# Decode attention beside an MLP on one core: the V loads of pairs 0 to 27 in ScalarE's own DMA queue, ScalarE's program written out

## The chip, the cores and the metric

The kernel runs on 1 of the 8 cores of one Trainium2 chip. A core has five engines with a program each: TensorE (PE in the profile; PEld is its weight load), VectorE (DVE), ScalarE (ACT), GpSimd (POOL) and SyncE (SP), and 16 DMA engines which move data between HBM and the on-chip memory SBUF. The metric is the device time of one execution in microseconds (us).

## The reference

One decode step: attention over a cache of 4096 keys for 8 batches and 32 heads, beside a small MLP on the same normalised input.

```python
# x: [8, 1, 640]; k_cache, v_cache: [8, 32, 4096, 128] bf16
def _A_ref(x, k_cache, v_cache, wq, wo):
    q = (x @ wq).reshape(B, Sq, Hq, Dh).transpose(0, 2, 1, 3)
    scores = jnp.einsum("bhqd,bhkd->bhqk", q, k) * (Dh ** -0.5)
    p = _softmax(scores, axis=-1)
    o = jnp.einsum("bhqk,bhkd->bhqd", p, v)
    return o.transpose(0, 2, 1, 3).reshape(B, Sq, Hq * Dh) @ wo
def _B_ref(x, w1, b1, w2, b2):
    h = _gelu(_layernorm(x) @ w1 + b1)
    return h @ w2 + b2
xn = _layernorm(x)
return x + _A_ref(xn, k_cache, v_cache, wq, wo) + _B_ref(xn, w1, b1, w2, b2)
```

The two caches are 537 MB, the weights 15 MB. Each byte of the caches is used once.

## The kernel before

The work is cut into 32 pairs i = 0 to 31: a group of 8 heads and one batch (`hq, b = divmod(i, 8)`). A pair's K and its V are one load each of 8.39 MB: 128 partitions (8 heads times 16 blocks of keys) of 256 keys of 128 numbers, 64 KB in each partition. SBUF has room for three such tiles in `S_sb`: slots KA and KB take K of even and of odd pairs, and slot VS takes every V. So two K loads can be under way or in use at a time, and one V.

For each pair the scores of the first 176 keys of a partition come from DVE in three chunks (`dve_chunk`: a multiplication by the broadcast query `qbc_sb`, which ScalarE copies from PSUM in `act_qbc`, a halving addition, a sum). The other 80 keys go through PE: `pe_T` transposes them in ten tiles, `act_T` copies each tile out of PSUM, `pe_QK` multiplies, `dve_sel` picks the own head. `k_ready` is a small POOL instruction that waits for the K load and releases PE. `dve_max` makes the maximum, `act_exp` (ScalarE, eight exps) the probabilities, `pe_RS` and `dve_rinv` the sums of them. `pe_PV` (256 matmuls) needs the V load and the probabilities; `act_O` copies its result to `oU_sb`, and `o_norm` on POOL scales it. After pair 31 the selected heads are multiplied by `wo` and the result is stored.

The order on every engine comes from positions: `at(pos, fn, i)` puts a step at a place, the steps are sorted by it, and each engine's instructions are recorded in that order. Pair i begins at i * 100. The places that matter: `load_k(i)` at -51, `act_qbc(i)` at -10.5, `act_T(i)` from 0 to 42, `load_v(i)` at +50, and, for the pair before, `pe_PV(i - 1)` at +50 and `act_O(i - 1)` at +71; `act_exp(i)` is at +90. On ScalarE the order is thus: evictions of pair i, oU copy of pair i - 1, query copy of pair i + 1, exps of pair i. On PE: transposes and scores of pair i, PV of pair i - 1, the query broadcast `pe_qbc` of pair i + 1.

All K and V loads are issued by SP, so they stand in one DMA queue, in SP's order: K of pair i + 1, V of pair i, K of pair i + 2, and so on. `load_k(i)` (line 350) waits until PE and DVE have read the K of pair i - 2; `load_v(i)` (line 362) waits for the end of PV of pair i - 1, since V has one slot. The last V is cut in four pieces. ScalarE issues three small loads at the start (x and the biases) and the store at the end.

SP's and POOL's programs are written out (`_replay`, line 116). DVE and ScalarE run pairs 2 to 31 as a loop of 15 turns of two pairs (`replay`, line 845, and `_replay_loop`, line 151): the recorded turns are compared, and semaphore waits get a register that grows with the turn. PE has a loop of its own (`_replay_pe`). As every instruction is emitted by `_emit`, the profile gives line 111 for all of them; they are told apart by their tiles.

Of the kernel before, what the change touches and what calls it, by code (L numbers as in the profile page):

```python
# [104 lines left out]
def _emit(e, call, wait=None, turn=None):  # L105
    name, a, k, inc = call
    a = [x.at(x.i if turn is None else turn) if isinstance(x, _Slot) else x for x in a]
    if name == "wait_ge":
        e.wait_ge(a[0], a[1] if wait is None else wait, **k)
        return  # L110
    inst = getattr(e, name)(*a, **k)  # L111
    if inc is not None:
        inst.then_inc(*inc)


def _replay(e, calls):
    for call in calls:
        _emit(e, call)
# [32 lines left out]
def _replay_loop(e, calls, a, b, n):  # L151

    size = (b - a) // n
    assert size * n == b - a and n >= 2
    _replay(e, calls[:a])
    grow = _steps([calls[a + r * size:a + (r + 1) * size] for r in range(n)])
    with e.bass.Fori(0, n, engines=OrderedEngineSet([e.engine])) as r:
        for call, step in zip(calls[a:a + size], grow):
            _emit(e, call, call[1][1] + r * step if step else None)
    _replay(e, calls[b:])  # L160
# [31 lines left out]
def bass_parallel_sum__gqa_block_cached__mixer_channel_mlp__decode_kernel(  # L192
# [11 lines left out]
    out: bass.AP,  # L204
):
    B, _, D = A_x.shape
    _, H, SK, DH = A_k_cache.shape
    F = B_w1.shape[1]
    assert DH == P and D % P == 0 and B == 8 and H % 8 == 0 and SK % P == 0
# [4 lines left out]
    NQ = NHQ * B  # L214
# [4 lines left out]
    TPB = 8  # L219
    NS = 2  # L220
    LOOP0, LOOPN = 2, 15
    assert NKEY == 256 and NQ == 32
    SLOT = NKEY * DH
    KA, KB, VS = 0, 1, 2
# [5 lines left out]
    def jp_of(i):  # L230
        return 80
# [16 lines left out]
    with ExitStack() as es:  # L248
# [6 lines left out]
        tile = [S_sb[:, s, :].rearrange("p (j d) -> p j d", d=DH) for s in range(3)]  # L255
# [72 lines left out]
        pe, dve, act, sp, pool = (_Eng(sem(f"{n}_s")) for n in ("pe", "dve", "act", "sp", "pool"))  # L328
        pe2, act2 = _Eng(sem("pe2_s")), _Eng(sem("act2_s"))
        ld_s = [_Dma(sem(f"ld_s{s}")) for s in range(3)]  # L330
# [6 lines left out]
        tk = {}  # L337
        prog = []

        def at(pos, fn, *a):  # L340
            prog.append((pos, len(prog), fn, a))
# [4 lines left out]
        def cache_src(cache, i):  # L346
            hq, b = divmod(i, B)
            return cache[b, hq * HS:(hq + 1) * HS].rearrange("h (p j) d -> (h p) j d", j=NKEY)
# [11 lines left out]
            tk[("k", i)] = ld_s[s].sig(sp.dma_start(tile[s][:, lo:hi, :], cache_src(A_k_cache, i)[:, lo:hi, :]))  # L360

        def load_v(i):
            sp.wait(tk["mlp"] if i == 0 else tk[("pv" if i < NQ - 1 else "pvh", i - 1)])
            if i < NQ - 1:
                tk[("v", i)] = [ld_s[VS].sig(sp.dma_start(tile[VS], cache_src(A_v_cache, i)))]
                return
            tk[("v", i)] = []
            for d, lo, hi in zip([ld_s[VS]] + ld_vl, V_CUT[:-1], V_CUT[1:]):
                if lo:
                    d.n += 1  # L370
                    sp.wait(tk[("pv", i - 1)])
                tk[("v", i)].append(
                    d.sig(sp.dma_start(tile[VS][:, lo:hi, :], cache_src(A_v_cache, i)[:, lo:hi, :])))
# [406 lines left out]
        for i in range(NQ):  # L780
            o = i * Q
            last = i == NQ - 1
            if i:
                at(o - 51, load_k, i)
            at(o + 50, load_v, i)
            at(o - 52, qrep, i)
            at(o - 2, k_ready, i)
            at(o - 11, pe_qbc, i)
            at(o - 10.5, act_qbc, i)
            nt = jp_of(i) // TPB  # L790
            w = 42.0 / nt
            for t in range(nt):
                at(o + w * t, pe_T, i, t)
                at(o + w * (t + 0.4), act_T, i, t)
                at(o + w * (t + 1.5), pe_QK, i, t)
            at(o + 2, dve_chunk, i, 0)
            at(o + 26, dve_chunk, i, 1)
            at(o + 52, dve_sel, i, 0)
            at(o + 55, dve_sel, i, 1)
            at(o + 58, dve_chunk, i, 2)  # L800
            at(o + 84, dve_max, i)
            at(o + 90 if i else o + Q + 45, act_exp, i)
            at(o + Q + 48, pe_RS, i)
            at(o + Q + 57, dve_rinv, i)
            at(o + Q + 50, pe_PV, i)
            if not last:
                at(o + Q + 71, act_O, i)
            at(o + Q + 75, o_norm, i)
# [3 lines left out]
        o = NQ * Q  # L812
# [10 lines left out]
            at(o + 5 if n == 0 else o + 79.2, pe_sel3, n)  # L823
            at(o + 5.5 if n == 0 else o + 79.5, dve_fold3, n)
        at(o + 90, fin_store)
        engs = {"dve": dve, "act": act}
        marks = {n: [] for n in engs}
        for m in range(LOOPN + 1):
            for n in engs:
# [12 lines left out]
        for _, _, fn, a in sorted(prog, key=lambda t: (t[0], t[1])):  # L842
            fn(*a)

        def replay(e, n):
            m = marks[n]
            assert len({y - x for x, y in zip(m, m[1:])}) == 1, (n, m)
            _replay_loop(e, engs[n].calls, m[0], m[-1], LOOPN)

        @block.sync  # L850
        def _(e):
            _replay(e, sp.calls)
# [9 lines left out]

        @block.scalar
        def _(e):
            replay(e, "act")

        @block.gpsimd
        def _(e):
# [29 lines left out]
```

## Time and profile before

| | us |
|---|---|
| median of 3 runs (1283.54 to 1283.78) | 1283.76 |
| the profiled execution | 1283.81 |
| its span, first to last instruction | 1281.8 |
| PE busy | 671.3 (52%) |
| DVE busy | 1095.1 (85%) |
| ScalarE busy | 475.1 (37%) |
| POOL busy | 88.7 (7%) |

The DMA engines moved 551.99 MB at a mean of 431 GB/s. Queue q1 is SP's and carried 551.79 MB; q10 is ScalarE's and carried 0.03 MB. Times in the views below are microseconds from the start of the span. A row of the chain gives start, duration and what; a row of the timeline gives start, duration, engine, operation, output and inputs, and in brackets how long the engine was idle before it and what released it. `SPq` and `ACTq` are DMA issues: their duration is that of the issue, not of the transfer.

### The profile page before, as it was taken

Reading aid. Unit: us, or ns where it says so; the run is one execution under the profiler, and the core shown is the slowest. Engines: PE = TensorE matmul, PEld = TensorE weight load, DVE = VectorE, ACT = ScalarE, POOL = GpSimd, SP = SyncE. Lnnn points to the kernel's source line nnn. Section 1 sums busy time; section 2 is a strip of 40 time slices with the busy share of each in tenths; the row PEclk is TensorE's granted clock in tenths of the full one; section 3 lists DMA queues with packets and bytes.
Section 4 is the critical chain, followed back from the end, with each engine's and each line's share of the span. In section 5 each row is a group of like instructions: output and inputs, shape, how many; then the busy total and the mean of one; then the engine's idle time right before and its main releaser. Section 6 shows DMA issues by size and latency. Waiting matters only on the chain.

```text
span 1281.8 us, 34444 instructions
## 1 busy us (share of the span) xinstructions
PE 671.3 (52%) x13944; PEld 575.0 (45%) x13944; DVE 1095.1 (85%) x675; ACT 475.1 (37%) x904; POOL 88.7 (7%) x108
## 2 busy tenths in 40 slices
PE   4365554564544564544664644654545655545645
PEld 4254443453443553433553534543434544434545
DVE  1799988988888988888988888988889988889885
ACT  1344432344432344423344423344323344323441
POOL 0001000000000000000000000000000000000001
PEclk9955655566655656555655555565555555555555
DMA  9999999999999999999999999999999999999998
GB/s 396 436 439 424 442 427 438 427 442 427 436 429 442 427 436 429 442 427 434 432 442 427 434 432 440 429 434 432 440 430 432 432 442 429 432 432 442 429 417 369
DMA packets 11235, 551.99 MB, mean 431 GB/s; under 512 B 1292, under 2 KB 1493, under 8 KB 1878
## 3 DMA queue, kind: packets, MB, share of 16 engines
q1 hardware_dynamic: 11152, 551.79, 99.7%
q8 instruction: 9, 0.15, 0.0%
q10 hardware_dynamic: 70, 0.03, 0.0%
q14 instruction: 4, 0.03, 0.0%
HBM read 551.80 MB, written 0.01 MB: 430 GB/s over the span
## 4 chain that ended last, share of the span: by engine, by line
DMA 80%; PE 19%; ACT 1%; issue 1%; SPq 0%; another core or an unknown queue 0%; DVE 0%; POOL 0%; ACTq 0%
DMA S_sb<-in_A_v_cache_dram 74%; PE PV_ps L111 17%; DMA S_sb<-in_A_k_cache_dram 3%; DMA S_sb<-in_A_wo_dram 2%; DMA S_sb<-in_B_w_dram 2%; PE TR_ps L111 1%; PE CH_ps L111 1%; ACT P_sb L111 0%; PE ACC_ps L111 0%; SPq L111 0%; PE S_ps L111 0%; ACT KT_sb L111 0%; PE QB_ps L111 0%; ACT S_sb L111 0%
## 5 line engine op out<-in xcount | busy, mean ns | idle before, releaser
L111 PE MATMUL TR_ps<-ident_bf,S_sb 128*128 128x128 bf16 (+1 forms) x2570 | 341.5, 278 | 376.8 <-POOL kr_sb L111 366.0
L111 DVE TENSOR_TENSOR S_sb<-S_sb,qbc_sb 128x7552 bf16<-128x7552 bf16 (+1 forms) x96 | 388.8, 4050 | 136.8 <-DMA S_sb<-in_A_k_cache_dram 136.8
L111 PEld LDWEIGHTS TR_ps<-ident_bf,S_sb 128*128 (+2 forms) x2570 | 244.8, 103 | 434.6 <-issue 360.3
L111 DVE TENSOR_REDUCE Sd_sb<-S_sb 128x59 f32<-128x3776 bf16 (+1 forms) x96 | 390.2, 4065 | 6.0
L111 ACT ACTIVATE KT_sb<-TR_ps 128x1024 bf16<-128x1024 bf16 x320 | 326.9, 1023 | 125.6 <-PE TR_ps L111 115.5
L111 PE MATMUL PV_ps<-P_sb,S_sb 128*128 128x8 bf16 x8192 | 224.0, 175 | 149.3 <-DMA S_sb<-in_A_v_cache_dram 146.2
L111 PEld LDWEIGHTS PV_ps<-P_sb,S_sb 128*128 128x128 bf16 x8192 | 221.2, 103 | 152.2 <-DMA S_sb<-in_A_v_cache_dram 149.0
L111 ACT ACTIVATE P_sb<-Sd_sb,NB_sb 128x256 bf16<-128x256 f32 x256 | 126.2, 494 | 218.5 <-DVE NB_sb L111 218.5
L111 DVE TENSOR_TENSOR S_sb<-S_sb 128x3776 bf16<-128x3776 bf16 (+1 forms) x96 | 202.9, 2114 | 3.3
L111 ACT ACTIVATE oU_sb<-PV_ps 128x8 f32<-128x8 f32 x31 | 5.5, 177 | 393.2 <-PE PV_ps L111 393.2
L111 PE MATMUL S_ps<-qrep_sb,KT_sb 128*128 128x8 bf16 x2560 | 122.0, 177 | 35.5 <-ACT KT_sb L111 31.8
L111 PEld LDWEIGHTS S_ps<-qrep_sb,KT_sb 128*128 128x128 bf16 x2560 | 91.8, 103 | 66.6 <-ACT KT_sb L111 39.5
L111 POOL TENSOR_TENSOR oT_sb<-oU_sb,ri_sb 128x8 bf16<-128x8 f32 x31 | 68.2, 2199 | 389.4 <-DVE S_sb L111 366.1
L111 ACT ACTIVATION_READ_ACCUMULATOR P_sb<-Sd_sb,NB_sb 128x1 f32 x256 | 47.7, 186 | 0.0
L111 POOL COPY qrep_sb<-qT_sb 128x128 bf16<-128x128 bf16 x32 | 14.5, 453 | 455.6 <-PE S_ps L111 435.8
L111 DVE TENSOR_TENSOR S_ps<-S_ps,mask_sb 128x320 f32<-128x320 f32 (+2 forms) x67 | 32.7, 488 | 4.3 <-PE S_ps L111 4.3
L111 DVE TENSOR_REDUCE Sd_sb<-S_ps 128x40 f32<-128x320 f32 x64 | 31.5, 492 | 2.2
L111 POOL MEMSET kr_sb<- 128x1 f32 x32 | 3.1, 98 | 324.0 <-DMA S_sb<-in_A_k_cache_dram 324.0
L111 PE MATMUL CH_ps<-rs_sb,ones_f 128*128 128x8 f32 x64 | 17.3, 344 | 9.9 <-DVE oS_sb L111 6.2
L111 PE MATMUL QB_ps<-ident_bf,qrep_sb 128*128 128x128 bf16 x32 | 9.1, 285 | 22.6 <-DVE S_sb L111 21.5
L111 PEld LDWEIGHTS CH_ps<-rs_sb,ones_f 128*128 128x128 f32 x64 | 15.1, 292 | 10.1 <-DVE oS_sb L111 6.3
L111 ACT ACTIVATE qbc_sb<-QB_ps 128x128 bf16<-128x128 f32 x32 | 8.8, 276 | 27.8 <-PE QB_ps L111 27.8
(57 smaller groups left out, 119.1 us busy)
## 6 DMA issues: line engine op xcount, KB each, us to landing
S_sb<-in_A_wq_dram SPq DMA_DIRECT2D x1, 5120.0 KB, 15.7
S_sb<-in_A_k_cache_dram SPq DMA_DIRECT2D x1, 4448.0 KB, 43.2
S_sb<-in_A_k_cache_dram SPq DMA_DIRECT2D x1, 3744.0 KB, 33.3
S_sb<-in_A_v_cache_dram SPq DMA_DIRECT2D x1, 3072.0 KB, 10.7
S_sb<-in_A_wo_dram SPq DMA_DIRECT2D x1, 2560.0 KB, 31.2
S_sb<-in_A_v_cache_dram SPq DMA_DIRECT2D x1, 2560.0 KB, 12.5
S_sb<-in_B_w_dram SPq DMA_DIRECT2D x1, 2160.0 KB, 20.4
S_sb<-in_B_w_dram SPq DMA_DIRECT2D x1, 2080.0 KB, 25.3
```

What stands on the lines that cost most here:

```text
L111: inst = getattr(e, name)(*a, **k)
```

## The change

`load_v(i)` of pairs 0 to 27 is issued by ScalarE, which waits for the same PV as SP did; V of pairs 28 to 31 stays with SP. The step moves from place +50 to +71.5 for these pairs, which is right behind `act_O(i - 1)` and ahead of `act_qbc(i + 1)` on ScalarE. ScalarE's instructions of different turns are no longer alike, so its program is written out like SP's; DVE keeps its loop. Loads, tiles, slots and semaphores are as before.

```diff
+    V_ACT = 28
@@
         def load_v(i):
-            sp.wait(tk["mlp"] if i == 0 else tk[("pv" if i < NQ - 1 else "pvh", i - 1)])
+            e = act if i < V_ACT else sp
+            e.wait(tk["mlp"] if i == 0 else tk[("pv" if i < NQ - 1 else "pvh", i - 1)])
             if i < NQ - 1:
-                tk[("v", i)] = [ld_s[VS].sig(sp.dma_start(tile[VS], cache_src(A_v_cache, i)))]
+                tk[("v", i)] = [ld_s[VS].sig(e.dma_start(tile[VS], cache_src(A_v_cache, i)))]
                 return
@@
-            at(o + 50, load_v, i)
+            at(o + (71.5 if i < V_ACT else 50), load_v, i)
@@
-        engs = {"dve": dve, "act": act}
+        engs = {"dve": dve}
@@
         @block.scalar
         def _(e):
-            replay(e, "act")
+            _replay(e, act.calls)
```

## The prediction

> **What bounds the kernel now.** I read the page first: how busy the DMA engines are, and whose waits end the chain.
>
> ```profile
> span 1281.8 us, 34444 instructions
> DMA  9999999999999999999999999999999999999998
> q1 hardware_dynamic: 11152, 551.79, 99.7%
> DMA 80%; PE 19%; ACT 1%; issue 1%; SPq 0%; another core or an unknown queue 0%; DVE 0%; POOL 0%; ACTq 0%
> ```
>
> The 16 DMA engines are full in every slice, with one queue, q1, which is SP's. The chain says "PE 19%", but that is the V slot being read between two V loads. The chain in order of time, one pair:
>
> ```profile
> 402.58 31.62 DMA S_sb<-in_A_v_cache_dram
> 434.20 0.05 issue
> 434.25 7.01 PE PV_ps L111 x256
> 441.26 0.02 issue
> 441.28 31.62 DMA S_sb<-in_A_v_cache_dram
> ```
>
> The period is 441.28 - 402.58 = 38.70 us. The timeline of the same stretch shows what the DMA engines do meanwhile:
>
> ```profile
> 402.58 0.33 SPq L111 DMA_DIRECT2D S_sb<-in_A_v_cache_dram  x1
> 402.58 0.18 ACT L111 ACTIVATE oU_sb<-PV_ps 128x8 f32<-128x8 f32 x1 [12.85 <-PE PV_ps L111]
> 403.43 0.28 ACT L111 ACTIVATE qbc_sb<-QB_ps 128x128 bf16<-128x128 f32 x1 [0.67 <-PE QB_ps L111]
> ...
> 409.12 0.33 SPq L111 DMA_DIRECT2D S_sb<-in_A_k_cache_dram  x1
> ...
> 414.89 0.10 POOL L111 MEMSET kr_sb<- 128x1 f32 x1 [9.88 <-DMA S_sb<-in_A_k_cache_dram]
> 414.97 4.03 DVE L111 TENSOR_TENSOR S_sb<-S_sb,qbc_sb 128x7424 bf16<-128x7424 bf16 x1 [4.27 <-DMA S_sb<-in_A_k_cache_dram]
> ...
> 443.68 4.09 DVE L111 TENSOR_REDUCE Sd_sb<-S_sb 128x59 f32<-128x3776 bf16 x1
> ...
> 447.84 0.33 SPq L111 DMA_DIRECT2D S_sb<-in_A_k_cache_dram  x1
> ...
> 453.60 0.10 POOL L111 MEMSET kr_sb<- 128x1 f32 x1 [9.87 <-DMA S_sb<-in_A_k_cache_dram]
> ```
>
> Landings: K 414.89, V 434.20, K 453.60, so 19.35 us each, strictly one after the other. V is asked for at 402.58, stands behind a K load with 12.3 us to go, and lands 31.6 us later. The next K is always asked for (409.12, 447.84) before the V ahead of it has landed, so the one queue never runs dry; during the 7 us of a PV, when no V load can be asked for, a K load is in flight. What bounds the kernel is 551.79 MB at this rate. Nothing can gain unless the rate rises; anything that leaves the DMA engines without a request is lost at full price. The working below therefore counts DMA idle time.
>
> **The change part by part.** E is the end of one PV, T the time to the next one.
>
> Issue moved from SP to ScalarE: SP loses 28 issues of 0.33 us, ScalarE gains them (its own three at the start took 0.61 and 0.54 for two). The new wait for pv stands right behind the oU copy, which waits for the same PV, so it delays nothing by itself. Behind it on ScalarE stand the qbc copy and the exps: qbc waits 0.67 us for PE anyway, which covers 0.33. V is asked for some 0.2 us later than now. Cost nothing; without the cover 28 x 0.33 = 9 us.
>
> K requests no longer stand behind V's wait on SP: they gain nothing. In the rows above K goes out at 447.84, right after the DVE reduce that frees its slot (443.68 + 4.09 = 447.77), 6.5 us after V's issue. DVE, not SP, times it.
>
> V 0 goes out behind ScalarE's evictions of pair 0, at about 61 us in place of 32.12. Then K 1 is in flight (lands 66.3 now) and K 2 is asked for at 71.38. V 0 fills in between: no idle time.
>
> ScalarE without a loop: the branch goes, some 900 instructions are gone through once each. The only idle time that can be code on its way is 3.10 us inside PE's first pass through PV, where PE goes through a matmul in 27 ns (7.00 us for 256). If one such stall fell ahead of every V issue, it cost 28 x 3.10 = 87 us. The nearer row is SP's: its program has no loop today, and its V issues stand 38.70 us apart with no exception; ScalarE has some 28 instructions a pair and waits 12.85 us before every oU, which covers a stall. I take nothing. The Trainium skill (Runtime: NRT & Kernel Launch, Instruction fetch mechanics) says that straight code is prefetched and the crossing mostly hidden; by it the sum is the same.
>
> Two queues in place of one order: this is the step that counts. Do the engines serve ScalarE's queue beside SP's? The first microseconds of the timeline show it:
>
> ```profile
> 0.73 0.38 SPq L111 DMA_DIRECT2D S_sb<-in_A_wq_dram  x1
> 0.74 0.61 ACTq L111 DMA_DIRECT2D S_sb<-in_A_x_dram  x1
> 1.39 0.54 ACTq L111 DMA_DIRECT2D S_sb<-in_B_b_dram  x2
> 2.40 0.87 DVE L111 BATCH_NORM_STATS2 S_sb<-S_sb 8x6 f32<-8x320 bf16 x2 [0.33 <-DMA S_sb<-in_A_x_dram]
> 11.02 0.19 PE L111 MATMUL ACC_ps<-S_sb 128*128 128x40 bf16 x1 [3.33 <-DMA S_sb<-in_B_b_dram]
> 16.46 4.43 PE L111 MATMUL CH_ps<-S_sb 128*128 128x8 bf16 x160 [4.89 <-DMA S_sb<-in_A_wq_dram]
> ```
>
> x, asked for after wq, is in use 1.7 us later; the small biases arrive at 11, before wq at 16.4. So the queues are served in turns, not by order of arrival. How large V's share is the rows don't say (x had hardly to wait, the biases 9 us for 4.6 KB); nothing favours one side, so I take half each. The Trainium skill (DMA: Bandwidth & Descriptors, Queues, rings and completion order) has each DMA engine go round-robin over queues packet by packet; that is the same half, if K and V packets are alike.
>
> Consequence: while both run, V needs up to 38.7 us in place of 19.35. K, which alone has the engines during the 7 us of PV and the start of V, gets 7.05 + 19.35 = 26.4 us of service in 45.8, more than the 19.35 it needs: a K load every 33.6 us, and DVE's 34.5 us a pair (414.97 to the end of its last row at 449.41) is then its limit. K's lead, 12 us short today, is made up in one or two pairs. K loads run ahead, until something else than K's landing holds DVE: the qbc copy. The qbc of pair i+1 comes after PV of pair i-1, so DVE starts a pair at E + 1.2 at the earliest (403.71 + 0.05 against 402.56). Today that is covered, for K lands only at 414.89; it is what is late next. From there: DVE takes 32.80 us to the last reduce (414.97 to 447.77), K is asked for at E + 34.1, and data flow at E + 35.7 (1.6 us from issue to arrival, as x; bounds 1.0, x from the end of its issue, and 3.6, wq's 15.7 to land against 12.1 of work at 19.35 us per 8.39 MB).
>
> Now the balance. K starts at E + 35.7. The next PV ends at E + T, and V's data start 1.8 later; until then K is alone for T - 33.9. Its rest, 19.35 - (T - 33.9) = 53.25 - T, is shared, and V is that much later than alone: V takes 19.35 + 53.25 - T. The next period is 1.8 + 72.6 - T + 7.05 = 81.45 - T. Equal periods: T = 40.7. Check: V lands at E + 33.65 and K starts at E + 35.7; the engines stand still for 2.05 us, and 38.7 + 2.05 = 40.75. The previous K has landed by then. So each of PV 1 to 26 has a hole of 2.05 us: 26 x 2.05 = 53 us. The shares drop out of it: V takes its own 19.35 and whatever K is served before V lands.
>
> Handover: V 28 is SP's again, with K 30 behind it in SP's order. At PV 27 K 29 has landed, K 30 can't be asked for, and the engines are idle for the whole PV and a start: 7.05 + 1.6 = 8.7 us. From there the order is today's.
>
> Sum: 53 + 9 = 62. The profiled execution took 1283.81 us, 0.05 above the median of 1283.76, with a span of 1281.8 and 2.0 around it: 1283.8 + 62 = 1346.
>
> Bounds. The start counts half in every hole and whole at the handover: 1.0 gives -8, 3.6 gives +28. The balance isn't damped (next period 81.45 - T): if a long and a short period alternate, say 46 and 36.5, the short one has a hole of 35.7 - (36.5 - 7.05) = 6.2 us and the long one none: 13 x 6.2 = 81 for 53, +28. With K served at two fifths V takes 32.3 us, K has 7.05 + 12.9 = 20.0 us in 39.3 and gains 1.2 us a pair, so the first ten holes are missing: -20.
>
> **Rivals.** *No change.* The Trainium skill (DMA: Bandwidth & Descriptors, Issuing engines are not separate DMA queues) says that spreading DMAs over issuing engines saves only issue time; by that 1283.8. As a mechanism here: the engines stay full if K never gets ahead. At a K share near three tenths, K gets 7.05 + 0.3 x 27.6 = 15.3 in 34.7 us, less than it needs, so K keeps holding DVE and a K load is in flight in every PV: 1284. For it: x came at once. Against: the biases took 9 us. 0.08.
>
> *Faster.* Two streams move more than one. The rate over a period is 16.78 MB / 38.70 = 433.5 GB/s; single 19 us stretches show up to 443. If the mix held 443 over 28 pairs, 1083 us become 1060: 1261. It has to be above 433.5 by more than the holes cost, 5%, or by 0.24% without holes. Against it: q1 is at 99.7% of the engines already. 0.05.
>
> *Much slower.* The mix loses rate: each per cent costs 11 us on top of 62; 5% gives 1400. ScalarE's stalls, if not covered, give up to 1346 + 87 = 1433. Nothing in the trace shows either. 0.07.
>
> **How the numbers follow.** Holes as worked out: 0.80, likeliest 1346, its own range 1318 to 1395 (1346 - 20 - 8 below; 1346 + 28 and most of the second 28 above). Leaving out no change, faster and most of much slower (0.08 + 0.05 + 0.07 = 0.2) the range is 1295 to 1395; its lower end, with some 12 us of holes left, takes in shares of K between two fifths and three tenths. Within 0.2% (2.6 us) is what a measurement of this kernel can't tell from no change. Faster 0.05; same 0.07; slower 0.88 (0.80, 0.07 and 0.01 of no change that isn't quite).
>
> **What would show it.** In the profile after: a DMA share below 1.0 in 7 us windows over PV; q1 and ScalarE's queue q10 near half of the bytes each; V landing after 30 to 36 us; K landing well before DVE uses it, DVE waiting for qbc (PE, ScalarE) and no longer for K; PV starts 40 to 41 us apart, or alternating around that; one period near 28 us after PV 27, then 38.7 again. K landings that still end DVE's waits would make the prediction wrong, towards no change; DMA engines that are full all the time with longer periods would mean a lost rate.

## The result and the profile after

| | us |
|---|---|
| before, median | 1283.76 |
| after, median | 1363.68 |
| ratio, with its 95% interval | 1.0619 (1.0603 to 1.0635) |
| span before, profiled execution | 1281.8 |
| span after, profiled execution | 1361.2 |

The change makes the kernel 6.2% slower, 79.9 us by the medians. (Two of the six runs after, 1394.63 and 1395.01 us, count as slow and are left out of the ratio; the other four, 1362.55 to 1363.90, give 79.5 us.) First the page of the kernel after, its span and its queues (packets, MB, share of 16 DMA engines over the span):

```profile
span 1361.2 us, 34023 instructions
q1 hardware_dynamic: 7120, 316.90, 55.4%
q10 hardware_dynamic: 4102, 234.91, 39.9%
```

The bytes are the same, split over two queues, and the shares add up to 95.3% where one queue had 99.7%. The timeline of the kernel after, through one period:

```profile
401.93 0.33 ACTq L111 DMA_DIRECT2D S_sb<-in_A_v_cache_dram  x1
402.77 0.28 ACT L111 ACTIVATE qbc_sb<-QB_ps 128x128 bf16<-128x128 f32 x1 [0.67 <-PE QB_ps L111]
403.07 4.03 DVE L111 TENSOR_TENSOR S_sb<-S_sb,qbc_sb 128x7424 bf16<-128x7424 bf16 x1 [5.96 <-ACT qbc_sb L111]
...
431.77 4.09 DVE L111 TENSOR_REDUCE Sd_sb<-S_sb 128x59 f32<-128x3776 bf16 x1
...
435.93 0.33 SPq L111 DMA_DIRECT2D S_sb<-in_A_k_cache_dram  x1
...
436.61 7.00 PE L111 MATMUL PV_ps<-P_sb,S_sb 128*128 128x8 bf16 x256 [16.73 <-DMA S_sb<-in_A_v_cache_dram]
...
443.65 0.18 ACT L111 ACTIVATE oU_sb<-PV_ps 128x8 f32<-128x8 f32 x1 [24.63 <-PE PV_ps L111]
443.65 0.33 ACTq L111 DMA_DIRECT2D S_sb<-in_A_v_cache_dram  x1
```

DVE is now released by the query copy and no longer by K's landing: 403.07 is 1.17 us after the end of PV at 401.90. Its last reduce ends at 435.86, K is asked for at 435.93, and V has landed at 436.57. At that moment the DMA engines have nothing on hand but a request 0.6 us old. The waits of the kernel after say the same for the whole run (who waited for what: us in total, times, longest):

```profile
DVE S_sb L111 <- ACT qbc_sb L111: 191.0, 28, 9.0
DVE S_sb L111 <- DMA S_sb<-in_A_k_cache_dram: 25.8, 3, 15.5
```

Before, the second row read 136.8 us in 30 waits. What the engines do when a V has landed is seen in windows of 5 us; the columns are from:to, length, busy time of PE, PEld, DVE, ACT and POOL, clock, DMA share and GB/s. Before, V landed at 472.90:

```profile
471.00:476.00 5.00, 3.06 (x114) 3.06 (x115) 4.93 (x5) 0.00 (x0) 0.00 (x0) 0.50 1.00 433
```

After, V landed at 477.33 in the first window, and V 27, the last one on ScalarE's queue, at 1218.99, just ahead of the second:

```profile
476.00:481.00 5.00, 3.62 (x135) 3.62 (x136) 3.09 (x7) 0.00 (x0) 0.00 (x0) 0.50 0.61 210
...
1219.00:1226.00 7.00, 6.97 (x256) 6.90 (x256) 1.33 (x6) 0.00 (x0) 0.00 (x0) 0.50 0.00 0
```

433 GB/s against 210: that is the hole; and at the handover nothing moves through a whole PV. (In windows as short as these the DMA column is rough, since packets of 2.42 us lie across their edges.)

Where the 79.4 us of span went, from the ends of PV in the two chains: PV 1 ends 22.5 us later than before (154.16 for 131.65); the 26 periods to PV 27 have a mean of 41.23 us for 38.70, together 65.6; the period after it is 29.16 for 38.69, which gives 9.5 back; the tail takes 0.8. 22.5 + 65.6 - 9.5 + 0.8 = 79.4. Most of the 22.5 us is no loss of its own: K's loads are served ahead there while V waits. The trace's packet records (start, duration, size and queue of each DMA packet, which no view prints) give the other side of it. Counting for each moment which part of the 16 engines had no data packet under way, 65.1 us are lost in the kernel after and 4.2 before; and the packets that start after a hole take about 3.1 us for 64 KB in place of 2.42, worth another 18.4 us. 60.9 + 18.4 = 79.3. For one hole of the long middle that is some 1.8 us without a packet and 0.7 of slow packets. The first ones differ: 2.2 us more than before are lost up to the end of PV 0, and 4.0 in the period that ends with PV 1.

### The profile page after: what moved, and what is told of

Read it like the earlier page. It is cut to its first block, busy times and chain, and to the rows that moved or that the text cites. A ratio compares the mean times of both kernels' runs of the same rounds, so it can differ in the third digit from the quotient of the medians.

```text
span 1361.2 us, 34023 instructions
## 1 busy us (share of the span) xinstructions
PE 675.9 (50%) x13944; PEld 575.0 (42%) x13944; DVE 1095.1 (80%) x675; ACT 465.9 (34%) x904; POOL 24.0 (2%) x108
## 4 chain that ended last, share of the span: by engine, by line
DMA 82%; PE 16%; ACT 1%; issue 1%; SPq 0%; DVE 0%; POOL 0%; ACTq 0%
DMA S_sb<-in_A_v_cache_dram 77%; PE PV_ps L111 16%; DMA S_sb<-in_A_k_cache_dram 3%; DMA S_sb<-in_A_wo_dram 2%; ACT KT_sb L111 1%; SPq L111 0%; PE TR_ps L111 0%; PE ACC_ps L111 0%; PE S_ps L111 0%; PE QB_ps L111 0%; ACT out_sb L111 0%; DVE res_sb L111 0%; ACT oU_sb L111 0%; POOL kr_sb L111 0%; ACTq L109 0%
## 5 line engine op out<-in xcount | busy, mean ns | idle before, releaser
L111 PE MATMUL TR_ps<-ident_bf,S_sb 128*128 128x128 bf16 (+1 forms) x2570 | 341.5, 283 | 64.6 <-POOL kr_sb L111 39.5
L111 ACT ACTIVATE KT_sb<-TR_ps 128x1024 bf16<-128x1024 bf16 x320 | 323.2, 1021 | 99.6 <-PE TR_ps L111 91.3
L111 PEld LDWEIGHTS S_ps<-qrep_sb,KT_sb 128*128 128x128 bf16 x2560 | 92.3, 103 | 146.8 <-DVE S_sb L111 83.6
L111 POOL TENSOR_TENSOR oT_sb<-oU_sb,ri_sb 128x8 bf16<-128x8 f32 x31 | 11.0, 355 | 706.7 <-ACT oU_sb L111 694.6
L111 POOL COPY qrep_sb<-qT_sb 128x128 bf16<-128x128 bf16 x32 | 9.5, 295 | 546.6 <-PE S_ps L111 527.2
L111 PE MATMUL CH_ps<-S_sb 128*128 128x8 bf16 (+1 forms) x244 | 12.0, 181 | 5.1 <-DMA S_sb<-in_A_wq_dram 4.4
## 6 DMA issues: line engine op xcount, KB each, us to landing
S_sb<-in_A_wo_dram SPq DMA_DIRECT2D x1, 2560.0 KB, 31.6
```

## The experiments

My theory: the engines serve the two queues in turns, K runs ahead until the query copy, behind PV, holds DVE, and a hole opens at every PV since K is then asked for too late. Rivals: ScalarE's written-out program; a loss that two queues make in themselves; something that happens once.

**ScalarE's program alone.**

```diff
-    V_ACT = 28
+    V_ACT = 0
```

> All V loads issued by SP again, ScalarE's program still written out without a loop. Theory (the holes come from the two queues): as before, 1283.8 us within 2, V loads 38.70 us apart. Rival (the loss is ScalarE's code on its way, or its program form): most of the 80 us stays, around 1340 to 1365.

Measured: 1287.94 us, ratio 1.0034 (1.0022 to 1.0047). So the form of the program isn't the cause of the 80 us, but it isn't free either, which the theory had missed. The chain of this run shows where the 4.2 us are:

```profile
441.37 31.63 DMA S_sb<-in_A_v_cache_dram
473.00 0.05 issue
473.04 7.01 PE PV_ps L111 x256
480.05 0.02 issue
480.06 32.32 DMA S_sb<-in_A_v_cache_dram
```

Single V loads take 32.3 us in place of 31.6, and little else changes. The page counts 12 code packets in queue q14, 4 before; in the packet records one of them lies in each of the seven longer periods (one 0.35 us longer, six 0.67 to 0.69). Three others, in the periods that end with PV 3, 12 and 23, cost nothing.

**DVE's program written out instead**, with the kernel before and ScalarE's loop as it was:

```diff
-        engs = {"dve": dve, "act": act}
+        engs = {"act": act}
@@
-                replay(e, "dve")
+                _replay(e, dve.calls)
```

> The kernel before, with DVE's program written out in place of ScalarE's; every load as before. If the 4.2 us of the run with ScalarE's program written out are code on its way through the DMA engines (there 7 code packets beyond pair 5 stood in the 7 periods that were 0.35 to 0.69 us longer), DVE, with some 21 instructions a pair for 28, has 4 to 6 such periods: 1286 to 1288. Rival (something of ScalarE's own, its waits or its copies): 1283.8 within 1.

Measured: 1287.78 us, 1.0032 (1.0020 to 1.0043). Nine code packets, and four periods of 39.66 to 39.68 and one of 38.89, for 38.70. So the cost follows written-out code, not ScalarE; the longer step in the chain is the load itself. How one code packet of 8 KB makes a load that 16 engines share 0.7 to 1.0 us longer can be read from the last whole V load, of pair 30, behind which there is little left to load. In the kernel before, its last 16 packets end 0.5 to 2.2 us ahead of the landing. With ScalarE's program written out, one packet ends 0.5 us ahead of the landing, the one before it 2.4 us earlier, as on one engine in sequence, and all others are through 4.8 us or more ahead of it; with DVE's written out, 4.5 us or more. So one engine has fallen behind the rest by some 4 us, about the whole loss, while the others went on to the next loads. The records don't name the engines. But read this way a code packet costs time only where the engine that ends last has served it, which fits the packets that cost nothing, here and in the kernel before (two in its long middle).

**Half the pairs.**

```diff
-    V_ACT = 28
+    V_ACT = 14
```

> V loads of pairs 0 to 13 alone go through ScalarE's queue, 14 to 31 through SP's. Theory (one hole per PV while K is ahead, and one hole of a whole PV at the handover): the loss of 79.9 us falls by 14 holes of 41.23 - 38.70 = 2.53 us, so 79.9 - 35.4 = 44.5: 1328 us. After the handover, periods of 38.70 at once. Rival (something that happens once, at the start or at the handover): the loss stays near 80. Rival (a cost that needs all pairs, ScalarE's code): near 80 too.

Measured: 1330.3 us, 1.0400 (1.0340 to 1.0461); after the handover 29.18, then 38.70 again (39.4 to 39.6 in places, as with the written-out program alone). One of the four runs took 1345.16 us, the others 1329.9 to 1330.46. The loss is one per pair (33.4 us less for 14 pairs less, 2.4 each) and not one event; some 13 us of it don't grow with the pairs.

**K in two halves.**

```diff
-            lo, hi = K_CUT[1:3] if i == 0 else (0, NKEY)
-            tk[("k", i)] = ld_s[s].sig(sp.dma_start(...))
+            for lo, hi in [K_CUT[1:3]] if i == 0 else [(0, NKEY // 2), (NKEY // 2, NKEY)]:
+                tk[("k", i)] = ld_s[s].sig(sp.dma_start(...))
```

> As the change, but each K load of pairs 1 to 31 is issued as two loads of half the keys back to back, so K's pieces are 32 KB a partition and V's stay 64 KB. Theory (the DMA engines take one piece of each queue in turn, 2.42 us for a 64 KB piece): K's share beside V is a third in place of a half. V then takes about 29 us in place of 34, K gets 7 + 29/3 = 16.7 us of service in 36, less than its 19.35, so K no longer runs ahead, DVE waits for K landings again, a K load is under way in every PV: 1284 to 1290 us, with no hole at the handover either. Rival (queues share by bytes or by load): the share stays a half, 1355 to 1370. Rival (two queues lose time in themselves, by mixing): 1340 to 1365.

Measured: 1322.56 us, 1.0294 (1.0277 to 1.0311). Neither theory nor rivals: half of the loss is gone, the periods are 40.18 us. My expectation forgot V's own start. K is alone not for 7 us but for some 11 (in the packet records V's first packets come 3.6 to 4.1 us after its issue), and so K still is done soon after V lands. DVE still waits for the query copy (22 times, 125.9 us), K is still asked for 34 us after PV, and by then the K before it is just running out. The hole is shorter, not gone.

**V in two halves.**

```diff
-                tk[("v", i)] = [ld_s[VS].sig(e.dma_start(tile[VS], cache_src(A_v_cache, i)))]
+                for lo, hi in [(0, NKEY // 2), (NKEY // 2, NKEY)]:
+                    tk[("v", i)] = [ld_s[VS].sig(e.dma_start(...))]
```

> As the change, but each V load is issued as two loads of half the keys, so that V's pieces are 32 KB a partition and K's stay 64 KB: K's share beside V is two thirds. Theory as the prediction put it (the share drops out: V takes its own 19.35 us and whatever K is served before V lands, and K is asked for 34 us after the end of PV at any share): a hole like the change's, 1352 to 1372 us. Rival (the share sets the loss, as the run with K in halves, 38.8 us in place of 79.9, may be read): a larger loss than the change's, 1390 or more.

Measured: 1374.52 us, 1.0724 (1.0670 to 1.0779); the profiled execution took 1365.29, its periods have a mean of 41.27. A hole like the change's, and no larger loss per pair in the profile. But the four runs are spread from 1365.29 to 1380.96, the median is 2.5 us above the range of the theory, and what the two runs of 1380 lost no profile shows.

**Both in halves.** The edits of the last two together. (With V in halves the first piece of the last V is cut in two as well.)

> As the change, but both the K loads and the V loads are issued as two loads of half the keys: pieces of 32 KB on both sides, share a half again, and K asked for in one go as late as in the change. It tells whether the run with K in halves (1322.6) gained by the share or by the smaller piece. Theory (turns by piece; the holes depend on K being done before V lands and asked for too late): as the change, 1352 to 1375 us. Rival (smaller pieces themselves help, for instance since the engines start anew faster): 1315 to 1330 as with K in halves.

Measured: 1364.77 us, 1.0631 (1.0613 to 1.0648), as the change. So the gain with K in halves was the share, not the smaller piece. The issue tables say how the turns go (loads, KB each, median us from issue to landing). First the change, then K in halves, then V in halves:

```profile
S_sb<-in_A_k_cache_dram SPq DMA_DIRECT2D x31, 34.0
...
S_sb<-in_A_v_cache_dram ACTq DMA_DIRECT2D x28, 34.1
```

```profile
S_sb<-in_A_k_cache_dram SPq DMA_DIRECT2D x62, 4096.0 KB, 35.4
...
S_sb<-in_A_v_cache_dram ACTq DMA_DIRECT2D x28, 33.0
```

```profile
S_sb<-in_A_v_cache_dram ACTq DMA_DIRECT2D x56, 4096.0 KB, 29.2
...
S_sb<-in_A_k_cache_dram SPq DMA_DIRECT2D x31, 28.1
```

The side with the whole pieces is served sooner, V at 33.0 and K at 28.1. (The rows of 4096 KB mix first and second halves.) In the packet records of the change the two queues alternate: about 2.4 us mostly of one, then 2.4 us mostly of the other.

**The query early.** Broadcast and copy of the next pair's query ahead of PV (the main lines; the edit also adds the broadcasts that this order needs at the end and moves part of the final selection):

```diff
-            at(o - 11, pe_qbc, i)
-            at(o - 10.5, act_qbc, i)
+            at(o - 51, pe_qbc, i)
+            at(o - 50.8, act_qbc, i)
```

> As the change, but the query broadcast of the next pair stands ahead of PV on PE, and its copy ahead of the oU copy on ScalarE, so that DVE's start no longer hangs on the end of PV (two broadcasts more than needed at the end, and part of the final selection 1 to 2 us later). Theory (the hole is there because K is asked for 34 us after the end of PV): DVE may start up to a period earlier, K is asked for earlier, the holes mostly go: some 10 us for the first pairs and the handover stay, 1293 to 1308. Rival (the holes come from the V slot alone, or from mixing two queues): no change, 1355 to 1368.

Measured: 1322.44 us, 1.0291 (1.0271 to 1.0312). The direction is the theory's and half of the loss goes, but not the size. The waits of this run show what is late next: DVE's step on the scores from PE, which in PE's order come behind PV as well.

```profile
DVE S_ps L111 <- PE S_ps L111: 137.2, 42, 5.2
...
PE TR_ps L111 <- POOL kr_sb L111: 92.8, 32, 15.5
```

In the kernel before, the first row stood at 4.3 us. The second gate lets the periods alternate around 36.3 and 42.8, with a hole in every second one.

**K asked for early.** K in two parts, the first (117 keys) asked for as soon as DVE's first two chunks are through and PE has been released (the main lines; `kc` is the end of a chunk on DVE, `kr` that of `k_ready`):

```diff
             if i >= 2:
-                sp.wait(tk[("kt", i - 2)], tk[("km", i - 2)])
+                sp.wait(tk[("kc", i - 2, 1)], tk[("kr", i - 2)])
@@
+            for lo, hi in [K_CUT[1:3]] if i == 0 else [(0, chunks(i)[1][1]), (chunks(i)[1][1], NKEY)]:
+                if i >= 2 and lo:
+                    sp.wait(tk[("kt", i - 2)], tk[("km", i - 2)])
```

> As the run with K in halves, but the first part (117 of 256 keys) is asked for as soon as DVE has done its first two chunks of the pair that holds the slot, at E + 1.2 + 20.6 = E + 21.8 in place of E + 34; the rest as now. Against the run with K in halves (1322.6) only the time of the request differs, and pieces of 30 and 35.6 KB in place of 32. Theory (a hole opens where K is asked for too late to be under way when V lands): K's data flow from E + 24.4, V lands near E + 33, no holes; what stays is ScalarE's code (4), the first pairs and the handover (up to 9): 1288 to 1302. Rival (the loss with halves comes from sharing or mixing, not from the time of K's request): 1318 to 1326 as with halves.

Measured: 1300.72 us, 1.0135 (1.0117 to 1.0153), in the theory's range. This is the run that decides. DVE still starts behind the query copy, at 698.86 after a PV that ended at 697.62:

```profile
690.63 6.99 PE L111 MATMUL PV_ps<-P_sb,S_sb 128*128 128x8 bf16 x256 [14.04 <-DMA S_sb<-in_A_v_cache_dram]
...
697.66 0.34 ACTq L111 DMA_DIRECT2D S_sb<-in_A_v_cache_dram  x1
...
698.86 4.03 DVE L111 TENSOR_TENSOR S_sb<-S_sb,qbc_sb 128x7424 bf16<-128x7424 bf16 x1 [4.37 <-ACT qbc_sb L111]
```

But the window around this V's landing, like the one that showed 210 GB/s above, is full, and the same window in the run with K in halves (V landed at 578.68) is not. First this run, then that one:

```profile
689.30:694.30 5.00, 3.67 (x138) 3.68 (x138) 4.79 (x7) 0.00 (x0) 0.00 (x0) 0.50 1.07 456
...
577.40:582.40 5.00, 3.68 (x138) 3.68 (x139) 3.66 (x7) 0.00 (x0) 0.00 (x0) 0.50 0.75 269
```

Two queues, a written-out program, the same gate, and periods of 38.8 from the sixth on, in places up to 39.5. Only the time of K's request differs from the run with K in halves, nearly, as the pieces are 30 and 35.6 KB for 32. By the packet records the engines lose at most 0.3 us in each of the periods that end with PV 1 to 26. The loss per pair is the hole.

**The same to pair 30.** The last edit with V_ACT = 31.

> As the run with K's first part asked for early (1300.7), but V of pairs 28 to 30 goes through ScalarE's queue too, so that no load of K stands behind a V's wait in SP's order. Theory (8.5 us of that run's 17 are the handover, when SP waits for the end of PV 27 with K 30 behind it and nothing is under way): 1290 to 1296, with a gap of some 3 us at most where SP takes over for the last V. Rival (the 17 us come with the mixed stretch itself): 1301 to 1303.

Measured: 1303.43 us, 1.0153 (1.0136 to 1.0170). Missed: the handover moved and didn't vanish. The time alone would fit the rival nearly as well; the windows decide. With V_ACT at 31 the engines run dry at PV 29 and 30, in windows of this run:

```profile
1235.00:1245.00 10.00, 9.17 (x266) 8.30 (x262) 7.71 (x8) 2.67 (x11) 0.24 (x2) 0.50 0.47 172
...
1265.00:1275.00 10.00, 7.00 (x256) 6.91 (x256) 9.93 (x5) 0.18 (x1) 0.30 (x2) 0.50 0.42 157
```

K is ahead, so there is no K left to load while PE reads the V slot for these pairs. I read the 8.5 us at the handover as the price of having let K get ahead, wherever it is paid.

**Half a PV.** Every second matmul of PV is left out, and with it half of the products with V; the loads are the same (the main line; the mark of the last matmul moves with it).

```diff
-            for j in range(NKEY):
+            for j in range(0, NKEY, 2):
```

> As the change, but PV multiplies every second key only, 128 matmuls in place of 256: half of the products of V are left out, the loads are the same. PV then takes 3.5 us. Theory (the period is half of 38.75 + PV + the time at which K's data start after the end of PV; 41.23 with PV = 7.05 gives 36.66 for the last): 39.5, a hole of 0.78 in place of 2.53. 26 x 0.78 = 20, and 14 for the rest (handover, ScalarE's code) less 3.5: 1314 us, 1308 to 1320. Rival (the loss belongs to two queues in flight, by mixing or restarts): 1350 to 1365.

Measured: 1334.14 us, 1.0368 (1.0304 to 1.0433). A shorter PV takes 30 us off, against the rival; the theory's 1314 was 20 too low. The four runs are spread from 1324.18 to 1339.89; the profiled one took 1339.41, and its timeline shows what it lost:

```profile
586.73 0.33 SPq L111 DMA_DIRECT2D S_sb<-in_A_k_cache_dram  x1
...
593.18 3.59 PE L111 MATMUL PV_ps<-P_sb,S_sb 128*128 128x8 bf16 x128 [22.44 <-DMA S_sb<-in_A_v_cache_dram]
...
629.78 3.58 PE L111 MATMUL PV_ps<-P_sb,S_sb 128*128 128x8 bf16 x128 [14.96 <-DMA S_sb<-in_A_v_cache_dram]
630.88 0.33 SPq L111 DMA_DIRECT2D S_sb<-in_A_k_cache_dram  x1
```

Long and short periods alternate, 45.0 and 36.3. In the long one K is asked for 6.4 us before V lands and there is no hole; in the short one 1.1 us after, and the packet records have 2.4 to 2.8 us without any packet in such periods. The mean is 40.65 for the 39.5 of equal periods.

## Why the prediction was right, and where its sizes were off

It forecast 1346 in a range of 1295 to 1395, slower with 0.88; measured 1363.68.

*What bounds the kernel:* right. Everything that cost time did so as idle or slow time of the DMA engines.

*The queues are served in turns, half each:* right: K takes 34.0 and V 34.1 us from issue to landing, and pieces of half the size move the balance the way that turns by piece would. That the engines go round-robin over the queues by packet is the rule of the Trainium skill (DMA: Bandwidth & Descriptors, Queues, rings and completion order), and the traces agree with it. The Trainium skill's sentence that issuing from several engines only saves issue time (DMA: Bandwidth & Descriptors, Issuing engines are not separate DMA queues), weighed as "no change", doesn't hold for this kernel: 1.0619. The loads do interleave on the same engines; what it leaves out is that the order of landings changes, and with it what waits for what.

*K runs ahead, and the query copy holds DVE:* right in place and number. E + 1.2 was forecast for DVE's start and 1.17 measured; E + 34.1 for K's request and 34.03 measured.

*The hole:* 2.05 us forecast, 2.53 measured. The term that was mis-sized is the start of K after its request: 1.6 was taken, and with the measured mean period the same balance gives 2 x 41.23 - 45.8 - 34.03 = 2.6, inside the bounds of 1.0 to 3.6. The packet records say what it consists of, in the mean of the 16 engines: they are through with V 0.7 us before V counts as landed, K's first packets start 1.2 us after the request, and they take 3.1 us for 2.4. (V's data were taken to start 1.8 us after PV; their first packets came 4.3 to 4.6 us after it, but this term drops out of the balance.) 26 x 0.5 = 13 of the 18 us that the forecast fell short.

*V 0 and the holes before PV 1's:* put at nothing, and that was wrong. V 0, asked for at 57.62, landed at 97.95, and then the engines ran short too: of the rest of the 18 us, 2.2 were lost up to the end of PV 0 and some 2 in a hole at PV 1 that was larger than the others.

*The share drops out:* right where K lands before V (K at half and at two thirds: periods of 41.23 and 41.27), wrong where it doesn't (K at a third: 40.18).

*The handover:* 8.7 us forecast; in the packet records 8.4 us without any packet, 9.0 in the mean of the engines; the next period 28 and 29.16.

*ScalarE without a loop at nothing:* wrong. The cover named for it, the 12.85 us that ScalarE waits, covers ScalarE, but the cost is in the loads: 4.2 us alone. The Trainium skill (Runtime: NRT & Kernel Launch, Instruction fetch mechanics) calls the crossing mostly hidden; here a code packet costs up to 0.7 us with ScalarE's program and 1.0 with DVE's, others cost nothing, and the measurement decides. How much of it is left inside the change, where holes may take it up, wasn't measured.

*The balance isn't damped:* in the change alternating periods (42.8 and 40.2) die out within a dozen pairs; in the runs with a shorter PV and with the query early they stay. With the shorter PV the mean of 40.65 against 39.5 makes 30 us in 26 periods, so an extra of the size of the 28 us is possible, but it didn't come in this run. The pair of 46 and 36.5 that the 28 us rest on doesn't quite fit its own balance: behind 46 it gives 35.45, and 46 + 36.5 = 82.5, where four loads and a hole of 6.2 us make 83.6.

## What to carry to other kernels

One queue of a kernel that is bound by DMA is also its schedule: a second queue gives each load a share at once, the load with more to spare runs ahead, and the first dependency that its lead uncovers then times its next request. Before a load moves to another queue, find the moment when the moved load can't be in flight (here PV, with one V slot), and ask whether the other queue surely has work then, with its next request as late as its dependencies allow. Where the engines are full, a program written out is also traffic.

## What the runs showed of the hardware that I had not expected

A program written out cost 4.2 us on ScalarE and 4.1 on DVE, though both engines wait often: single loads became 0.2 to 1.0 us longer, each with a code packet of 8 KB in its time, and at the end one of the 16 DMA engines was some 4 us behind the others. After an idle stretch of the DMA engines the first packets of 64 KB took about 3.1 us in place of 2.42, so that a hole costs some 0.7 us more than its length.
